# Order of the split products in the expert blocks, and branch hints from the fourteenth block on

## The chip, the cores and the metric

The kernel runs on one core of a Trainium2 chip, as one program. The metric is the time of one execution on the device in microseconds; a version is told by the median of its runs. A profiled execution gives the span from its first to its last instruction and the rows that are quoted here. The engines are TensorE (PE for its products, PEld for its weight loads), VectorE (DVE), ScalarE (ACT), GpSimd (POOL) and SyncE (SP, which issues most DMAs). A "q" behind an engine's name means its sequencer, which waits, branches and issues.

## The reference

Three layers follow each other. The attention has no softmax; each score goes through a sigmoid.

```
scores = scale * q @ k.T - log(S)            # 4 batches, 12 heads, 448 x 64
x = sigmoid(scores) @ v                      # then reshaped to 1792 tokens x 768
idx = argmax over 8 experts of cosine(x, expert_emb) / tau;  gate = its softmax weight
for e in range(8):                           # w1[e]: 768 x 1024, w2[e]: 1024 x 768
    m = idx == e
    x2[m] = gate[m] * (relu(x[m] @ w1[e]) @ w2[e])
out = ((x2 @ w_a) * (x2 @ w_b)) @ w_out      # 768 x 1536, 1536 x 768
```

Which expert a token goes to is known only when the kernel runs.

## The kernel before

Every product of full precision is made from three products of TensorE in a shorter format: each operand is split into a high and a low part (`split`, lines 759 to 761: ScalarE copies the high part, VectorE subtracts it from the operand to get the low part), and high x high, high x low and low x high are summed in PSUM.

The work has three stages. The attention (`attention`) runs over batches and pairs of heads and, beside them, routes the tokens to experts. The expert stage (`moe`) works on blocks of 128 tokens of one expert each. The last stage (`glu`) multiplies groups of 512 tokens by `w_a`, `w_b` and `w_out`; its rows carry the names `ab` and `o`. The order in which every engine gets its instructions is that of the Python text.

The tokens come in two phases of 896, so 14 blocks at least are live, and a phase can need more, up to 28 in all: every expert rounds its tokens up to full blocks. Blocks 0 to 13 always run. Each later block stands in a `tc.If` on the value `live`, nested in the block before it (`block`, line 979); `live` is loaded into a register on all engines a block ahead. In the profiled execution 18 blocks run: 288 weight loads per kind of product at line 906, 16 to a block. Where the first block is not live, each engine branches to the arm for that case, takes a few semaphore steps there, and branches on to the code of the last stage.

One block (`block1`) does this on TensorE:

- `p1_half`, twice: 18 products of 512 columns for one half of `h` (lines 820 to 822), a ReLU on ScalarE (line 823). In the second one, after four of six steps, `h_tr(b, 0)` transposes the first turn of `h` (line 869) into PSUM, and ScalarE and VectorE make `hTh` and `hTl`, its high and low parts, from it.
- `p2`, the second product: for each of eight slices `kk`, three kinds of products with two column halves each: `hTh` x `w2h`, `hTh` x `w2l`, `hTl` x `w2h` (line 906, tile `p`). Between its slices stand `h_tr(b, 1)`, the transposes of the second turn of `h`, which gives the other four slices of `hTh` and `hTl`, and `x_load(b + 1)`, which transposes the next block's tokens (line 756).
- Where the next block has another expert (`chg`), the splits of its `w1` are issued behind `x_load`, four of the eight splits of `w2` behind this block, and the other four in the next block, around its two `p1` (`was_new`). Block 0 splits the last four slices of its own `w2` behind its `x_load`.
- VectorE scales the two halves of `p` by the gate into `y` (line 949), and GpSimd scatters `y` to memory (line 955).

In `glu`, `y_tr` transposes the tokens of the first group (line 756, tile `py`), ScalarE and VectorE split them into `yh` and `yl`, and the first `ab` products (lines 1071 to 1073) need those and the split weights `whi` and `wlo`. Beside all stages a preparation of `w_a`, `w_b`, `w_out` runs in small units (`prep_tick`, lines 195 to 212).

Of the kernel before, what the change touches and what calls it, by code (L numbers as in the profile page):

```python
# [20 lines left out]
ENGINES = [ET.SP, ET.Activation, ET.DVE, ET.PE, ET.Pool]  # L21
# [3 lines left out]
def build(ctx: ExitStack, tc: tile.TileContext, q, k, v, emb, tau, w1, w2, wa, wb, wo, out, dbg=None, stop=None):  # L25
# [16 lines left out]
    KF = DF // P  # L42
# [183 lines left out]
    def prep_tick(dma=nc.sync, behind=0):  # L226
        prep_store(dma)
        prep_finish(behind)
        prep_load(next_unit[0] + 3, dma)
        prep_unit()  # L230
# [220 lines left out]
    def pump(ps=(True, LATE, END)):  # L451

        while bg:
            job = next((j for j in bg if j[2]), bg[0])
            if job[1] and job[1] not in ps:
                return
            job[2] = False
            try:
                job[1] = next(job[0])
                return  # L460
            except StopIteration:
                bg.remove(job)
# [300 lines left out]
    def fl(b, row):  # L763
        ph = 0 if b < LIVE0 else 1
        return flg[ph][0:1, row, b - TB[ph][0]:b - TB[ph][0] + 1]

    def value(b, row, mx, engines):
        return nc.values_load(fl(b, row), engines=engines, min_val=0, max_val=mx)

    def load_w(which, expert, pair):  # L770
        t, src = (r1[pair], w1) if which == 1 else (r2[0][:, 2 * pair:2 * pair + 2, :], w2)
        nc.sync.dma_start(out=t, in_=src[expert, 2 * pair * P:2 * (pair + 1) * P, :].rearrange("(k p) c -> p k c", p=P))

    def split_w(which, kk, pool=None):
        hi, lo = (w1h, w1l) if which == 1 else (w2_t["h"], w2_t["l"])
        t = r1[kk // 2][:, kk % 2, :] if which == 1 else r2[0][:, kk, :]
        split(hi[kk], lo[kk], t, hi[kk].bitcast(F32))

    def gather(b):
        if b >= NBLK:  # L780
            return
        ph = 0 if b < LIVE0 else 1
        t = xg_t[b % len(xg_t)]
        j = b - TB[ph][0]
        nc.gpsimd.indirect_dma_start(out=t, out_offset=None, in_=xs_d[:CAP[0], :] if ph == 0 else xs_d[:, :],
                                     in_offset=bass.IndirectOffsetOnAxis(ap=idx[ph][:, j:j + 1], axis=0))
        xg[b] = t
# [26 lines left out]
    def p1_half(b, hf, ps, h, inner, at=4):  # L814
        xh, xl = xT_[b]
        cs = slice(hf * FH, (hf + 1) * FH)
        for kk in range(KD):
            if kk == at:
                inner()
            nc.tensor.matmul(ps, lhsT=xh[:, kk, :], rhs=w1h[kk][:, cs], start=kk == 0, stop=False)  # L820
            nc.tensor.matmul(ps, lhsT=xh[:, kk, :], rhs=w1l[kk][:, cs], start=False, stop=False)  # L821
            nc.tensor.matmul(ps, lhsT=xl[:, kk, :], rhs=w1h[kk][:, cs], start=False, stop=kk == KD - 1)  # L822
        nc.scalar.activation(out=h, in_=ps, func=AF.Relu)
        hs_of.setdefault(b, []).append(h)
# [40 lines left out]
    def h_tr(b, hf):  # L865
        px = misc["ps"]()
        n = FH // P
        for kk in range(n):
            nc.tensor.transpose(out=px[:, kk * P:(kk + 1) * P], in_=hs_of[b][hf][:, kk * P:(kk + 1) * P],
                                identity=ident)  # L870
        ks = slice(hf * n, (hf + 1) * n)
        split(hT["h"][:, ks, :], hT["l"][:, ks, :], px.rearrange("p (k c) -> p k c", k=n),
              hT["h"][:, ks, :].bitcast(F32))

    def moe(r2_p):
        pool = moe_pool
        w2h, w2l, hTh, hTl = w2_t["h"], w2_t["l"], hT["h"], hT["l"]
        mx_p = pool("mx", 2)
        r2.append(r2_p.tile([P, KF, DM], F32, name="r2"))
        ps_1 = pool("ps_1", 2, space=PSUM)  # L880
        ps_2 = pool("ps_2", 2, space=PSUM)
        ps_x = pool("ps_x", 4, space=PSUM)
        misc["ps"] = lambda: ps_x.tile([P, 512], F32, tag="px", name="px")
        def block1(b, chg, was_new, load, e_load):
            def when_new(fn, chg=chg):
                if chg is not None:
                    with tc.If(chg == 1):
                        fn()

            def load_new(which):  # L890
                for i in range((KD if which == 1 else KF) // 2):
                    load_w(which, e_load, i)

            def split_new(which, k0, k1):
                for kk in range(k0, k1):
                    split_w(which, kk)

            def p1(hf, inner):
                p1_half(b, hf, ps_1.tile([P, FH], F32, tag="p1", name="p1"),
                        mx_p.tile([P, FH], F32, tag="h", name="h"), inner)  # L900

            def p2(yp, k0, k1):
                for kk in range(k0, k1):
                    for l, wv in ((hTh, w2h), (hTh, w2l), (hTl, w2h)):
                        for hf in range(2):
                            nc.tensor.matmul(yp[hf][:, :HD], lhsT=l[:, kk, :], rhs=wv[kk][:, hf * HD:(hf + 1) * HD],  # L906
                                             start=kk == 0 and wv is w2h and l is hTh,
                                             stop=kk == KF - 1 and l is hTl)

            def tick():  # L910
                if b < LIVE:
                    pump()
                    pump()

            if b > 0:
                when_new(lambda: load_new(1), load)
                p1(0, lambda: None)
                when_new(lambda: split_new(2, KF // 2, KF - 2), was_new)
                tick()

                def rest():
                    h_tr(b, 0)
                    when_new(lambda: split_new(2, KF - 2, KF), was_new)

                p1(1, rest)
                tick()
                if b < LIVE - 1:
                    prep_tick(behind=1)
                when_new(lambda: load_new(2), load)
            yp = [ps_2.tile([P, 512], F32, tag="p2", name="p2") for _ in range(2)]  # L930
            p2(yp, 0, 1)
            h_tr(b, 1)
            p2(yp, 1, 2)
            x_load(b + 1)
            if b == 0:
                split_new(2, 4, KF)
                when_new(lambda: load_new(1), load)
                when_new(lambda: load_new(2), load)
            when_new(lambda: split_new(1, 0, KD))
            p2(yp, 2, KF // 2)  # L940
            gather(b + 2)
            tick()
            if 0 < b < LIVE - 1:
                prep_tick(behind=1)
            p2(yp, KF // 2, KF)
            tick()
            y = mx_p.tile([P, DM], F32, tag="y", name="y", bufs=1)
            for hf in range(2):
                nc.vector.tensor_scalar(out=y[:, hf * HD:(hf + 1) * HD], in0=yp[hf][:, :HD],
                                        scalar1=slots[:, 2, b:b + 1], scalar2=None, op0=ALU.mult)  # L950
            when_new(lambda: split_new(2, 0, KF // 2))
            ph = 0 if b < LIVE0 else 1
            j = b - TB[ph][0]

            nc.gpsimd.indirect_dma_start(out=ys_d if b < LIVE else ys_d[:Y0, :], out_offset=bass.IndirectOffsetOnAxis(ap=idy[ph][:, j:j + 1], axis=0),
                                         in_=y, in_offset=None)

        for i in range(2, KF // 2):
            load_w(2, e_of[0], i)

        def block(b, was_new=None):
            nx = b + 1
            if nx < NBLK:
                if b + 2 >= LIVE0:
                    while bg:
                        pump()
                chg = value(nx, 1, 1, [ET.Activation, ET.DVE, ET.Pool])
                load = value(b + 2, 3, 1, [ET.SP])
                e_load = value(b + 2, 4, E - 1, [ET.SP])
                live = value(nx, 0, 1, ENGINES) if nx >= LIVE else None  # L970
            else:
                chg = load = e_load = None
            block1(b, chg, was_new, load, e_load)
            if nx == LIVE:
                first_loads()
            if nx < LIVE:
                block(nx, chg)
            elif nx < NBLK:
                with tc.If(live == 1):
                    block(nx, chg)  # L980

        block(0)
        moe_s.close()

# [222 lines left out]
```

## Time and profile before

| what | value |
|---|---|
| median of 3 runs | 1097.88 us (1095.52 to 1099.14) |
| the profiled execution's own time | 1095.02 us |
| its span, first to last instruction | 1093.3 us |
| TensorE busy with products | 1063.3 us, 97% of the span |
| VectorE, ScalarE, GpSimd busy | 595.8, 501.3, 152.5 us |
| mean granted clock of TensorE, as a share of full speed | 0.995 |

Busy shares are means over stages with different limits. A row of a wait tells which engine stood and whose result ended it; the idle time of an engine other than the one that sets the end costs nothing by itself. Products on TensorE overlap, so the distance from one row to the next tells more than the length in a row.

### The profile page before, as it was taken

The page shows a single profiled execution, that of the slowest core. Times are in us where ns is not written, and L with a number is a line of the kernel's source. Part 1 is how long each engine was busy: PE and PEld are TensorE (multiplying, and loading weights), DVE is VectorE, ACT ScalarE, POOL GpSimd, SP SyncE. Part 2 cuts the span into 40 slices and gives each one's busy share as a digit, 9 for nine tenths or more (in the row PEclk, how much of TensorE's full clock was granted, in tenths as well). Part 3 has the DMA queues.
Part 4 walks back from the last instruction along what each step waited for, and adds up shares of the span by engine and source line. Part 5 has one row for each costly group of instructions (what it writes and reads, how often), then busy time and mean ns, then how long its engine had stood idle before and what let it go on. Part 6 is the DMA issues. An engine that isn't in the chain of part 4 may idle for free.

```text
span 1093.3 us, 16706 instructions
## 1 busy us (share of the span) xinstructions
PE 1063.3 (97%) x5996; PEld 866.6 (79%) x5996; DVE 595.8 (54%) x1037; ACT 501.3 (46%) x761; POOL 152.5 (14%) x218
## 2 busy tenths in 40 slices
PE   7999999999999999999979999999999999999998
PEld 4555555599888888888968878888888888888997
DVE  2566788865883879271255996433333433333553
ACT  5777777442763676261243554332323322323443
POOL 2121322232121212131101331000000000000000
PEclk9999999999999999999989999999999999999999
DMA  6687687539658865722182665064221162220730
GB/s 164 168 210 204 174 237 213 197 138 338 243 211 305 326 226 211 299 82 110 45 287 67 245 213 230 1 242 177 87 87 44 59 268 107 88 87 1 317 132 29
DMA packets 116744, 187.69 MB, mean 172 GB/s; under 512 B 53784, under 2 KB 88856, under 8 KB 110624
## 3 DMA queue, kind: packets, MB, share of 16 engines
q1 hardware_dynamic: 112000, 171.10, 46.6%
q0 software_dynamic: 3040, 14.94, 3.7%
q8 instruction: 49, 0.80, 0.3%
q10 hardware_dynamic: 1600, 0.39, 0.2%
q14 instruction: 55, 0.45, 0.1%
HBM read 154.17 MB, written 32.24 MB: 170 GB/s over the span
## 4 chain that ended last, share of the span: by engine, by line
PE 43%; DVE 3%; DMA 2%; issue 1%; ACT 1%; POOL 0%; SPq 0%; ACTq 0%; DVEq 0%; POOLq 0%
PE ab L1071 10%; PE ab L1072 9%; PE ab L1073 9%; PE o L1104 5%; PE o L1105 5%; PE o L1106 5%; DVE wlo L761 1%; DMA wx<-wm 1%; DVE m L195 1%; DMA r<-wm 1%; PE ab L756 0%; DVE wx L212 0%; ACT whi L760 0%; DVE m L197 0%; POOL m L202 0%
## 5 line engine op out<-in xcount | busy, mean ns | idle before, releaser
L1071 PE MATMUL ab<-yh,whi 128*128 128x512 f32 (+1 forms) x576 | 210.2, 365 | 4.0 <-DVE m L1079 2.1
L1072 PE MATMUL ab<-yl,whi 128*128 128x512 f32 (+1 forms) x576 | 209.6, 364 | 0.0
L1073 PE MATMUL ab<-yh,wlo 128*128 128x512 f32 (+1 forms) x576 | 209.5, 364 | 0.0
L202 POOL TENSOR_TENSOR m<-m,raw 128x384 int32<-128x384 int32 x72 | 76.2, 1059 | 369.0 <-DVE m L197 162.4
L1071 PEld LDWEIGHTS ab<-yh,whi 128*128 128x128 f32 x576 | 109.2, 190 | 20.2 <-DVE m L1079 2.5
L1073 PEld LDWEIGHTS ab<-yh,wlo 128*128 128x128 f32 x576 | 109.1, 189 | 17.4 <-DVE wlo L761 0.2
L1072 PEld LDWEIGHTS ab<-yl,whi 128*128 128x128 f32 x576 | 109.1, 189 | 15.7
L1104 PE MATMUL o<-whi,gh 128*128 128x512 f32 x336 | 114.7, 341 | 0.0
L1105 PE MATMUL o<-whi,gl 128*128 128x512 f32 x336 | 113.9, 339 | 0.0
L1106 PE MATMUL o<-wlo,gh 128*128 128x512 f32 x336 | 112.9, 336 | 0.0
L1079 DVE TENSOR_TENSOR m<-ab,a 128x512 f32<-128x512 f32 (+1 forms) x48 | 30.0, 624 | 149.8 <-PE ab L1073 149.7
L760 ACT CAST gh<-m 128x512 fp32r<-128x512 f32 (+1 forms) x48 | 27.2, 567 | 173.6 <-DVE m L1079 173.6
L557 ACT ACTIVATE a<-ps,bias_s 128x896 f32<-128x896 f32 x96 | 92.7, 1004 | 27.4 <-PE ps L552 26.6
L761 DVE TENSOR_TENSOR wlo<-wx,whi 128x768 fp32r<-128x768 f32 x72 | 66.0, 972 | 46.8 <-ACT whi L760 46.7
L761 DVE TENSOR_TENSOR wlo<-r,whi 128x768 fp32r<-128x768 f32 x70 | 65.0, 984 | 45.9 <-ACT whi L760 45.9
L820 PE MATMUL p<-w1h,xh 128*128 128x512 f32 x216 | 86.2, 399 | 0.1
L822 PE MATMUL p<-w1h,xl 128*128 128x512 f32 x216 | 84.7, 392 | 0.0
L821 PE MATMUL p<-w1l,xh 128*128 128x512 f32 x216 | 84.4, 391 | 0.0
L906 PE MATMUL p<-w2h,hTl 128*128 128x384 f32 x288 | 74.1, 338 | 7.2 <-DVE hTl L761 7.2
L574 PE MATMUL av<-a,v 128*64 128x448 f32 (+1 forms) x384 | 78.4, 565 | 1.5 <-DVE xtok L590 1.5
L906 PE MATMUL p<-w2h,hTh 128*128 128x384 f32 x288 | 76.3, 346 | 0.0
L760 ACT CAST whi<-wx 128x768 fp32r<-128x768 f32 x72 | 55.4, 833 | 41.8 <-PE o L1105 35.5
(236 smaller groups left out, 1830.2 us busy)
## 6 DMA issues: line engine op xcount, KB each, us to landing
wx<-wm SPq DMA_DIRECT2D x22, 1152.0 KB, 12.3
r<-wm SPq DMA_DIRECT2D x21, 1152.0 KB, 7.1
r<-in_moe_w_dram SPq DMA_DIRECT2D x28, 768.0 KB, 7.6
r<-in_moe_w_dram SPq DMA_DIRECT2D x18, 1024.0 KB, 9.2
raw<-in_moe_w_a_dram SPq DMA_DIRECT2D x24, 384.0 KB, 5.1
raw<-in_moe_w_b_dram SPq DMA_DIRECT2D x24, 384.0 KB, 4.6
raw<-in_moe_w_out_dram SPq DMA_DIRECT2D x24, 384.0 KB, 3.5
wm<-ab SPq DMA_DIRECT2D x48, 192.0 KB, 5.6
```

What stands on the lines that cost most here:

```text
L557: nc.scalar.activation(out=a[r], in_=ps[:n, :, :S], func=AF.Sigmoid, bias=bias_s[:n], scale=qscale)
L761: eng.tensor_tensor(out=lo, in0=src, in1=f32_hi, op=ALU.subtract)
L820: nc.tensor.matmul(ps, lhsT=xh[:, kk, :], rhs=w1h[kk][:, cs], start=kk == 0, stop=False)
L821: nc.tensor.matmul(ps, lhsT=xh[:, kk, :], rhs=w1l[kk][:, cs], start=False, stop=False)
L822: nc.tensor.matmul(ps, lhsT=xl[:, kk, :], rhs=w1h[kk][:, cs], start=False, stop=kk == KD - 1)
L906: nc.tensor.matmul(yp[hf][:, :HD], lhsT=l[:, kk, :], rhs=wv[kk][:, hf * HD:(hf + 1) * HD], start=kk == 0 and wv is w2h and l is hTh, stop= ...
L1071: nc.tensor.matmul(ps[:, :n], lhsT=hi[:, s, cs], rhs=yh[:, kk, :n], start=kk == 0, stop=False)
L1072: nc.tensor.matmul(ps[:, :n], lhsT=hi[:, s, cs], rhs=yl[:, kk, :n], start=False, stop=False)
L1073: nc.tensor.matmul(ps[:, :n], lhsT=lo[:, s, cs], rhs=yh[:, kk, :n], start=False, stop=kk == KD - 1)
L1104: nc.tensor.matmul(t[:, d0:d1], lhsT=gh[:, cs], rhs=hi[:, 2, d0:d1], start=first, stop=False)
L1105: nc.tensor.matmul(t[:, d0:d1], lhsT=gl[:, cs], rhs=hi[:, 2, d0:d1], start=False, stop=False)
L1106: nc.tensor.matmul(t[:, d0:d1], lhsT=gh[:, cs], rhs=lo[:, 2, d0:d1], start=False, stop=last)
```

## The change

It has two parts. The slices of `p2` are issued in another order: in each half of four slices, all products with `hTh` come first and those with `hTl` behind them; `h_tr(b, 1)` stands behind the `hTh` products of two slices, `x_load` behind those of a third. And from the block on that the first conditional block follows, each engine gets a hint instruction at the start of a block, which names the branch at the block's end and gives the register `live` as what it will do; the `tc.If` names the body as the way that falls through.

```
-            def p2(yp, k0, k1):
+            def p2(yp, k0, k1, part=slice(0, 3)):
                 for kk in range(k0, k1):
-                    for l, wv in ((hTh, w2h), (hTh, w2l), (hTl, w2h)):
+                    for l, wv in ((hTh, w2h), (hTh, w2l), (hTl, w2h))[part]:
...
-            p2(yp, 0, 1)
+            p2(yp, 0, 2, slice(0, 2))
             h_tr(b, 1)
-            p2(yp, 1, 2)
+            p2(yp, 2, 3, slice(0, 2))
             x_load(b + 1)
...
             when_new(lambda: split_new(1, 0, KD))
-            p2(yp, 2, KF // 2)
+            p2(yp, 3, KF // 2, slice(0, 2))
+            p2(yp, 0, KF // 2, slice(2, 3))
             gather(b + 2)
...
-            p2(yp, KF // 2, KF)
+            p2(yp, KF // 2, KF, slice(0, 2))
+            p2(yp, KF // 2, KF, slice(2, 3))
...
                 live = value(nx, 0, 1, ENGINES) if nx >= LIVE else None
+                if live is not None:
+                    tc.mark_branch_hint_location(f"live{nx}", live, ENGINES)
...
             elif nx < NBLK:
-                with tc.If(live == 1):
+                with tc.If(live == 1, label=f"live{nx}", preferred_fallthrough_block=True):
                     block(nx, chg)
```

## Rows read from the trace of the kernel before

**Rows 1.** Waits, whole expert stage: who waited for whom, us in total, times, longest.
```profile
PE p L906 <- DVE hTl L761: 7.2, 6, 1.8
```
**Rows 2.** Timeline, 407 to 412: start, us, engine, line, operation, tiles, count, idle before.
```profile
407.70 0.51 PE L906 MATMUL p<-w2h,hTh 128*128 128x384 f32 x2
...
408.51 0.60 ACT L823 ACTIVATE h<-p 128x512 f32<-128x512 f32 x1
...
409.92 0.62 PE L906 MATMUL p<-w2h,hTl 128*128 128x384 f32 x2 [1.36 <-DVE hTl L761]
410.37 0.60 PE L869 MATMUL px<-ident,h 128*128 128x128 f32 x4
```
**Rows 3.** Windows of two pairs: length, then PE, PEld, DVE, ACT, POOL busy, clock, DMA.
```profile
410.65:429.21 18.56, 17.52 (x95) 15.65 (x93) 18.42 (x26) 16.04 (x24) 4.57 (x4) 1.00 0.70 268
296.28:315.72 19.44, 18.54 (x98) 16.22 (x98) 19.30 (x26) 14.81 (x22) 4.57 (x4) 1.00 0.73 277
```
**Rows 4.** Timeline, 426 to 430.6.
```profile
426.19 0.59 ACT L760 CAST hTh<-px 128x512 fp32r<-128x512 f32 x1 [0.50 <-PE px L869]
...
428.14 0.60 ACT L823 ACTIVATE h<-p 128x512 f32<-128x512 f32 x1
...
430.40 0.38 PE L869 MATMUL px<-ident,h 128*128 128x128 f32 x2
```
**Rows 5.** Timeline, 308.5 to 317.
```profile
308.89 0.56 ACT L201 ACTIVATE ab<-raw 128x384 f32<-128x384 bf16 x1 [3.10 <-DMA wm<-ab]
...
312.93 0.66 PE L869 MATMUL px<-ident,h 128*128 128x128 f32 x4 [0.76 <-ACT h L823]
...
316.17 0.61 ACT L823 ACTIVATE h<-p 128x512 f32<-128x512 f32 x1
...
316.91 0.27 PE L869 MATMUL px<-ident,h 128*128 128x128 f32 x1
```
**Rows 6.** Timeline of three other blocks.
```profile
372.29 0.61 PE L906 MATMUL p<-w2h,hTl 128*128 128x384 f32 x2 [1.38 <-DVE hTl L761]
...
484.20 0.59 ACT L823 ACTIVATE h<-p 128x512 f32<-128x512 f32 x1
...
485.39 0.60 PE L869 MATMUL px<-ident,h 128*128 128x128 f32 x4
...
223.69 3.57 DVE L761 TENSOR_TENSOR w2l<-r,w2h 128x768 fp32r<-128x768 f32 x4
...
228.63 0.39 PE L820 MATMUL p<-w1h,xh 128*128 128x512 f32 x1
```
**Rows 7.** Line 979, VectorE, 540 to 560: ns min/median/max, first and last start.
```profile
L979 DVEq COMPARE_BRANCH  x2: 47/52/56, 549.0 to 552.2; - x2
L979 DVEq EVENT_SEMAPHORE  x2: 21/21/21, 552.0 to 552.1; - x2
```
**Rows 8.** The chain that ended last, 548 to 557: start, us, what.
```profile
552.28 2.15 issue
```
**Rows 9.** Timeline, 547 to 563.
```profile
547.05 0.51 PE L906 MATMUL p<-w2l,hTh 128*128 128x384 f32 x2
547.39 0.51 PE L906 MATMUL p<-w2h,hTl 128*128 128x384 f32 x2
...
552.14 2.46 PE L756 MATMUL py<-ident_r,raw 128*128 128x128 f32 x21 [2.73 <-issue]
...
554.83 1.95 DVE L761 TENSOR_TENSOR yl<-py,yh 128x384 fp32r<-128x384 f32 x4 [5.92 <-ACT whi L760]
...
556.46 0.77 PE L1071 MATMUL ab<-yh,whi 128*128 128x512 f32 x1 [1.86 <-DVE yl L761]
...
562.45 0.59 ACT L1076 COPY a<-ab 128x512 f32<-128x512 f32 x1 [2.07 <-issue]
```
**Rows 10.** Window behind the expert stage, columns as in the third group.
```profile
554.00:559.50 5.50, 3.64 (x12) 2.80 (x12) 4.67 (x11) 5.17 (x11) 0.00 (x0) 0.50 1.03 397
```
**Rows 11.** Timeline, 655 to 658.
```profile
656.60 0.50 PE L1071 MATMUL ab<-yh,whi 128*128 128x512 f32 x1 [2.10 <-DVE m L1079]
```

## The prediction

> **What bounds the kernel now.** I read the page first: one execution spans 1093.3 us, its own time is 1095.02 us, and TensorE is busy for 97% of the span, so a change can only pay where TensorE stands still or runs at its lower clock. Then I listed TensorE's idle stretches from the first expert block to the end, by its timeline, and by the waits view who ended them. There are three kinds. In the expert blocks, six waits for `hTl`, 7.2 us together, the longest 1.8 [rows 1]. Behind the last two expert products (547.39+0.51, so 547.9) a gap of 8.5 us with only 24 transposes in it, up to the first GLU product at 556.46 [rows 9]. And one wait of 2.1 us in the GLU stage, at 656.60 [rows 11], in lines that the diff doesn't touch. So the prize is bounded: 7.2 us in the blocks, and some 8 us and the slow clock behind them.
>
> *The waits in the blocks.* In block 410 (blocks are named by the time of their wait) the products `p` begin at 407.70; where nothing is awaited, rows of two stand 0.34 to 0.35 us apart (547.05 and 547.39 [rows 9]), so a product takes 0.174. The first with `hTl` waits 1.36 us, and the transposes of the second turn of `h` come at 410.37, although `h` itself was done at 408.51+0.60=409.11 [rows 2]. VectorE makes `hTl` late because it still splits the new expert's weights: all six waits stand in blocks that follow a change of expert.
>
> *The gap behind the blocks.* Here the code of line 979 is the thing to read. VectorE's branch past the dead blocks starts at 549.0 (2 rows: 549.0 and 552.2) and takes 0.06 us; its next instruction, the semaphore step of the not-taken arm, is at 552.0 [rows 7]. The chain of waits then has 2.15 us of "issue" at 552.28, behind VectorE's second branch: no semaphore is waited for, the instruction is simply not there [rows 8]. TensorE, idle for 2.73 us, goes on at 552.14, just behind that step, ScalarE with it, VectorE's `yl` starts at 554.83, TensorE's first `ab` product at 556.46 [rows 9]. [...] So two fetches of code on VectorE, 2.9 and 2.2 us, set the start of the GLU stage.
>
> **The change, part by part.** *New order of the products.* Nothing is added: 48 products a block before and after, each with its own weight load, the two PSUM tiles in the same alternation. Eight products with `hTh` (instead of four, and two with `hTl`) stand ahead of the transposes `h_tr(b, 1)`, and the first `hTl` product comes behind 16 others and both sets of transposes, some 3.5 us into the stage. A block without a wait gains nothing: x_load keeps its place, 12 products in, and the gather its place behind the first 24. In a block with a wait, the transposes can start when the eight products are done or `h` is there (with 0.1 us of hand-over, as from 552.0 to 552.14), whichever is later, and two products more, 0.35 us, are then behind them. A restart costs up to 0.1 us per step (0.45 us from 409.92 to 410.37 where 0.35 is the rule); I take 0.15.
>
> Block 410: eight products end at 409.09, `h` gives 409.21; against 410.37 that is 1.16+0.35-0.15=1.4 us. But what is late next? Block 430 changes expert again, and from 410.65 to 429.21 VectorE is busy for 18.42 of 18.56 us [rows 3]. Its work doesn't come sooner when TensorE does, so what block 410 gains, TensorE would stand at 430. There `h` sets the end: 428.14 on ScalarE, less the 0.50 us that ScalarE waited for TensorE at 426.19, so 427.64+0.60+0.10=428.34 against 430.40 [rows 4]: 2.06+0.35-0.15=2.3 us for the two blocks together. Blocks 296 and 316 are such a pair too, VectorE busy for 19.30 of 19.44 us [rows 3]. There a store held ScalarE for 3.10 us at 308.89, TensorE waits for its `h` at 312.93 already, and the second `h` ends at 316.17+0.61=316.78 whatever TensorE does; the transposes now start at 316.91 [rows 5]: 0.03+0.35, 0.4 us. Block 372, with a wait of 1.38 us [rows 6], has no change of expert behind it: 1.4 us, as 410 by itself. Block 485: 484.20+0.59+0.10=484.89 against 485.39 [rows 6]: 0.50+0.35-0.15=0.7 us. One block loses: in block 0 the last four `w2l` are made while they are used, 3.57 us from 223.69, 0.89 each [rows 6]. Six products per `kk` take 1.04 us and stay behind that; four take 0.69 and overtake it. The last `w2l` is there at 227.26; two products and eight with `hTl`, 10x0.174, end at 229.0, and the next block now starts at 228.63 [rows 6]: a loss of 0.4 us. Sum: 0.4+1.4+2.3+0.7-0.4=4.4 us. Bounds: 7.2 us above [rows 1]; below 1.7, if both pairs give nothing.
>
> *The hints.* From the fourteenth block on there is one instruction more per block on each engine, and five of them execute. No row shows it. Nearest are VectorE's branches and semaphore steps, 0.02 to 0.06 us [rows 7], so 0.3 us on a queue; the other end is the 2.9 us that a branch waits for its code, should the instruction itself wait so. I take nothing, by the nearer rows: these blocks have no wait of TensorE except the one at 485, so VectorE and ScalarE have idle time that covers it. Without the cover it is 0.3 us.
>
> *What the hint is worth* if the code of the not-taken arm is there when VectorE branches: its semaphore step comes at 549.2, not 552.0, and the second branch at 549.4. [...] Then ScalarE starts `yh` at 549.3, and VectorE its `yl` one copy of 0.5 us later, at 549.85, and from `yl` to the first product it is 1.63 us, as now: 551.5, 5.0 us sooner. Late next is VectorE: from the point at which TensorE starts it still has two `wlo` and four `yl` to make, some 3.1 us (four take 1.95 [rows 9]), and TensorE at full clock would be there after 2.3: a wait of 0.8. In return the clock: the first 18 products take 6.0 us now (556.46 to 562.45, where ScalarE copies them); at full clock a product of 512 columns takes 0.213+0.014=0.227 (384 columns: 0.160 of the 0.174), 18 of them 4.1, with the wait 4.9. TensorE's idle stretches would be 1.3 and 0.4 us; the 1.36 us in block 410 left the clock at 1.00 [rows 2, 3], the 2.73 us before 552.14 did not, and these are nearer to the first. So 1.0 us for the clock, and 6.0 in all. Bounds: 0, and 7.4 us (556.46 less 549.05, the branch itself). What TensorE gains here it keeps, since VectorE's work in the GLU stage is started by TensorE's products.
>
> Together 4.4+6.0=10.4 us: 1095.0 becomes 1084.6. The profiled execution is 2.9 us under the median of the runs, 1097.88, so the median comes to **1087.5 us**.
>
> [...] The row at 552.28 shows an engine that waits for code behind a branch [rows 8]. [...] No row here has a hint in it.
>
> **The rivals.** *1. Only the first fetch goes.* For it: the gaps are two, and the second stands with the arm's code already there. `yl` starts 2.55 us behind the second branch (552.28 to 554.83), so at 549.4+2.55=551.95, 2.9 us sooner; TensorE would be idle for some 2.4 us before it, near the 2.73 that cost the clock and far from the 1.36 that didn't; half of the clock's 1.0 counts. 3.4+4.4=7.8 us: 1090.1.
>
> *2. The hint does nothing*, only the order counts: 1093.5. For it: no row shows code that comes ahead of a branch. Against it: the branch's value is known a whole block ahead.
>
> [...]
>
> **How the numbers follow.** Chances: forecast 0.43, rival 1 0.25, rival 2 0.20, rival 3 0.12. The forecast's own spread is some 3 us either way, from the pairs and the clock. The range takes in rivals 1 and 2 and the better part of the bound of 7.2 us in the blocks: **1083.5 to 1095.0**; left out are rival 3 and a tail, some 0.18. 0.3% is 3.3 us, about what a measurement of this kernel can tell from no change. Faster by that: forecast, rival 1 and half of rival 2, 0.78. Within it: the other half and a little of rival 3, 0.13. Slower: 0.09.
>
> **What would show it.** Right: no wait for `hTl` in blocks 296 to 485, waits for `h` in its place, large only in the second block of each pair; some 0.4 us for `w2l` in block 0; VectorE's step of the not-taken arm within 0.3 us of its branch, TensorE's first `ab` product 3.6 us behind the last expert product, and the granted clock at 1.00 through it. Wrong: still 3 us behind VectorE's branch (rival 2), 2 us behind its second (rival 1), or new idle time of TensorE in the last five blocks (rival 3). The sum also fails if the 2.1 us wait in the GLU stage grows by what its start gains.

## The result and the profile after

The changed kernel takes 1087.30 us (median of 4 runs, 1084.99 to 1090.51), the kernel before, run beside it, 1096.88 (4 runs, 1095.52 to 1099.14): a ratio of 0.9906, 95% interval 0.9884 to 0.9928. The forecast was 1087.5. That the sum came out does not make its terms right, so the terms come next.

The profiled execution of the changed kernel took 1089.07 us and spans 1087.31, that of before 1095.02 and 1093.31: 6.0 us apart, where the medians are 9.6 apart. By stage (from TensorE's timeline of both: first expert product with `w2h`, end of the last one, 19th `ab` product, end of the span) the 6.0 us are +1.31 ahead of that first product, -4.09 in the expert stage, -4.88 from there to the 19th `ab` product and +1.66 in the rest of the GLU stage. The change touches the two in the middle, 9.0 us against the 10.4 forecast. The two others go with stretches at the lower level of TensorE's clock (0.50), as the windows show (length, busy time of PE, PEld, DVE, ACT, POOL, granted clock, DMA):

```profile
548.10:551.30 3.20, 3.20 (x16) 2.60 (x15) 3.20 (x8) 3.20 (x9) 0.00 (x0) 0.50 0.84 281
551.50:554.50 3.00, 3.00 (x14) 2.44 (x14) 2.78 (x6) 1.24 (x2) 0.00 (x0) 1.00 0.97 393
650.50:653.70 3.20, 3.20 (x9) 2.53 (x8) 3.13 (x7) 3.19 (x6) 1.12 (x1) 0.50 0.44 181
...
201.00:206.00 5.00, 5.00 (x20) 2.90 (x22) 3.51 (x14) 1.48 (x2) 1.02 (x1) 0.50 0.02 9
```

The last window lies ahead of the experts; before, the clock was back at 1.00 there by 204.8. In the one from 650.5 TensorE runs nine products where at full clock it runs sixteen (in `b0_old`, below, over the same time). It stands behind the wait of [rows 11], which is 2.11 us now and was 2.10; before, the clock stayed at 1.00 behind it. The fourteen profiles of this study (before, after and twelve experiments) sort cleanly by it: the first product with `w2h` comes at 219.0 to 219.5 us where the low stretch ahead of the experts lasts 3.4 us, at 220.4 to 220.9 where it lasts 6.8; the rest of the GLU stage takes 531.1 to 531.2 us without a low stretch and 532.7 to 533.0 with one, whatever the change in the code.

*The blocks.* The waits view of the expert stage, to hold against [rows 1]:

```profile
PE px L869 <- ACT h L823: 1.1, 3, 0.5
PE px L869 <- ACTq L887: 1.0, 1, 1.0
PE p L821 <- DVE w1l L761: 0.3, 2, 0.2
```

No wait for `hTl` is left of the 7.2 us; beside them, before, stood 0.8 us for `h` (312.93 in [rows 5]). Now 2.4 us stand under other names, the largest a new one of 1.05 us in a block that had waited for nothing before, at 351.13. The timeline there:

```profile
339.48 0.56 ACT L199 ACTIVATE raw<-raw 128x384 int32<-128x384 uint32 x1 [0.17 <-ACTq L887]
349.12 0.55 ACT L201 ACTIVATE ab<-raw 128x384 f32<-128x384 bf16 x1 [9.08 <-DMA wm<-ab]
350.48 0.60 ACT L823 ACTIVATE h<-p 128x512 f32<-128x512 f32 x1 [0.82 <-ACTq L887]
...
351.13 0.66 PE L869 MATMUL px<-ident,h 128*128 128x128 f32 x4 [1.05 <-ACTq L887]
```

ScalarE stands for 9.08 us in front of its step `ab<-raw` (line 201, which prepares the GLU weights) until a store has landed, starts `h` 0.82 us behind that step, and TensorE waits for `h`. It is the kind of wait of [rows 5].

*The hand-over.* The timeline that answers to [rows 9], and VectorE's branch line (983 now) to hold against [rows 7]:

```profile
545.83 0.42 PE L756 MATMUL py<-ident_r,raw 128*128 128x128 f32 x3 [0.70 <-PEq L983]
547.02 2.38 PE L756 MATMUL py<-ident_r,raw 128*128 128x128 f32 x21 [0.78 <-PE py L756]
...
547.04 1.69 ACT L760 CAST yh<-py 128x384 fp32r<-128x384 f32 x4 [7.59 <-DVEq L983]
...
547.73 1.95 DVE L761 TENSOR_TENSOR yl<-py,yh 128x384 fp32r<-128x384 f32 x4 [1.60 <-ACT yh L760]
...
549.37 0.77 PE L1075 MATMUL ab<-yh,whi 128*128 128x512 f32 x1
...
554.54 0.39 PE L1075 MATMUL ab<-yh,whi 128*128 128x512 f32 x1
```

```profile
L983 DVEq COMPARE_BRANCH  x2: 61/70/79, 546.3 to 547.1; - x2
L983 DVEq EVENT_SEMAPHORE  x2: 21/21/21, 546.9 to 547.0; - x2
```

The step of the not-taken arm comes 0.6 us behind the start of the first branch, not 3.0, and `yl` starts 0.6 us behind the second branch, not 2.6. That code was on its way in both waits of before is in the trace: of the DMA packets of the kind `instruction` (on the page, 49 of 16 KB on one queue, 55 of up to 8 KB on another) one of 16 KB starts between 549.0 and 549.5 and two of 8 KB between 550.0 and 550.5, in the first wait, and one of 8 KB between 552.3 and 553.0, in the second. In the changed kernel none moves from 544.2 to 547.2, and two of 8 KB do between 547.26 and 547.73. For which engine a packet is, the trace does not tell. The last expert product ends at 545.13; the first `ab` product follows 4.24 us later (8.56 before), the 19th, at 554.54, 9.41 us later (14.29 before).

### The profile page after: what moved, and what is told of

It is laid out like the page before. It is cut to its first block, busy times and chain, and to the rows that moved or that the text cites. A ratio compares the mean times of both kernels' runs of the same rounds, so it can differ in the third digit from the quotient of the medians.

```text
span 1087.3 us, 16743 instructions
## 1 busy us (share of the span) xinstructions
PE 1066.4 (98%) x5996; PEld 866.6 (80%) x5996; DVE 594.7 (55%) x1037; ACT 501.5 (46%) x761; POOL 152.9 (14%) x218
## 4 chain that ended last, share of the span: by engine, by line
PE 44%; DVE 3%; DMA 2%; ACT 1%; issue 0%; POOL 0%; SPq 0%; ACTq 0%; POOLq 0%
PE ab L1075 10%; PE ab L1076 10%; PE ab L1077 10%; PE o L1108 5%; PE o L1109 5%; PE o L1110 5%; DVE wlo L761 1%; DMA wx<-wm 1%; DVE m L195 1%; DMA r<-wm 1%; PE ab L756 0%; DVE wx L212 0%; PE py L756 0%; ACT whi L760 0%; DVE m L197 0%
## 5 line engine op out<-in xcount | busy, mean ns | idle before, releaser
L760 ACT CAST whi<-wx 128x768 fp32r<-128x768 f32 x72 | 55.4, 832 | 44.2 <-PE o L1109 36.3
L760 ACT CAST whi<-r 128x768 fp32r<-128x768 f32 x70 | 53.8, 832 | 47.0 <-PE o L1109 42.5
```

Source lines behind the costliest of these rows:

```text
L760: nc.scalar.copy(out=hi, in_=src)
```

## The experiments

All ratios are to the kernel before on the same chip, with 95% intervals. In the tables, a block's length is the distance between the first `w2h` products of two blocks, and the hand-over goes from the end of the last expert product to the first `ab` product, both from TensorE's timeline.

**Each half by itself.** `order_only` is the changed kernel without the hints and with the plain branch; `hints_only` is the kernel before with them.

```diff
# order_only
-                if live is not None:
-                    tc.mark_branch_hint_location(f"live{nx}", live, ENGINES)
-                with tc.If(live == 1, label=f"live{nx}", preferred_fallthrough_block=True):
+                with tc.If(live == 1):
```

> The new order of the products alone, no hints. Theory (two parts that add up, the order worth about 4.1 us as the profile after the change shows it, the hints about 5): 1092.5 to 1093.5 us against some 1097, ratio about 0.996; the waits for hTl gone, the stage of the expert blocks some 4 us shorter, and the gap behind the last block as before: VectorE's next instruction 2.9 us behind its branch at the last live block, 2.2 us behind the next branch, 8.5 us from the last expert product to the first ab product. Rival (the order also shortens the gap, for instance by moving code): the gap under 7 us, ratio 0.993 or less.

> The hints alone, with the old order of the products. Theory: about 5 us less, ratio about 0.9955; six waits for hTl as before (7.2 us together), 4.3 us from the last expert product to the first ab product, VectorE's next instruction within 0.6 us of its branch. Rival (the hints cost something in the blocks, which the order hides): ratio 0.998 or more, new idle time of TensorE in the last five blocks.

`order_only`: 0.9943 (0.9927 to 0.9958), 1092.08 us. `hints_only`: 0.9951 (0.9937 to 0.9966), 1092.06 us. The product, 0.9894, lies within the interval of the two together, 0.9884 to 0.9928: the halves add, and neither is idle. The profiles part them cleanly. `order_only` has an expert stage of 324.58 us (changed kernel 324.72, before 328.80) and a hand-over of 8.69; `hints_only` has 328.66 and 4.24, and its waits view still has the six waits:

```profile
PE p L906 <- DVE hTl L761: 8.3, 6, 1.8
```

**Which hint counts.** `hint_dve_only` gives the hint to VectorE alone, `hint_not_dve` to every engine but VectorE, `hint_18_only` to all engines but only ahead of the first dead block.

```diff
# hint_dve_only
-                    tc.mark_branch_hint_location(f"live{nx}", live, ENGINES)
+                    tc.mark_branch_hint_location(f"live{nx}", live, [ET.DVE])
# hint_not_dve
+                    tc.mark_branch_hint_location(f"live{nx}", live, [e for e in ENGINES if e != ET.DVE])
# hint_18_only (and the plain branch for the other blocks)
-                if live is not None:
+                if nx == 18:
```

> The changed kernel, but the hint on VectorE alone. Theory (VectorE's two fetches of code set the start of the last stage, those of the other engines are hidden): within 1 us of the changed kernel, 1087 to 1088.5, although ScalarE, TensorE and SyncE still wait 2 to 4 us for code behind their branches. Rival (the late code of TensorE or ScalarE would be the next limit, just behind VectorE's): the first ab product 1 to 3 us later than in the changed kernel, 1088.5 to 1090.5.

> The changed kernel, but with one hint only, for the branch that is not live in this data (block 18), so that the code of each engine grows by one hint in front of that branch and not by one per block. Theory A (the hint brings the arm's code and what follows it): both of VectorE's waits for code are gone, 1087 to 1088. [...]

> The hint stays on four engines and is taken from VectorE alone. Theory A (the hand-over behind the experts is set by VectorE's two waits for code, and by nothing that the hint does on the other engines): VectorE's branch past the dead blocks is followed only some 2.9 us later and its second branch some 2.2 us later, as before the change (2.92 and 2.15), the first ab product comes some 8.5 us behind the last expert product instead of 4.24, and the time is that of the order alone, about 1092. Rival B (the hints on TensorE, ScalarE or SP also give something, or move code of VectorE): one of VectorE's two waits is gone or shorter, hand-over 6 us or less, 1087 to 1090.

`hint_dve_only`: 0.9890 (0.9875 to 0.9906), hand-over 4.24. (The 2 to 4 us of its text, in the trace of the kernel before: ScalarE's step of the arm comes 4.2 us behind its branch, 542.8 to 547.0, SyncE's 2.4, 505.6 to 508.0, and TensorE's branch takes 3.6.) `hint_18_only`: 0.9886 (0.9871 to 0.9902), hand-over 4.24. Both are the whole effect: the hint for one branch of five is enough, and so is VectorE's hint alone. `hint_not_dve` came out between its two expectations: 0.9929 (0.9908 to 0.9949), hand-over 6.75. VectorE's branch line there:

```profile
L983 DVEq COMPARE_BRANCH  x2: 47/52/56, 545.1 to 548.1; - x2
L983 DVEq EVENT_SEMAPHORE  x2: 21/21/21, 547.9 to 548.0; - x2
```

The first wait is back, from 545.1 to 547.9. The second is not, `yl` starting at 548.68 behind the branch at 548.1. So the first wait goes only with VectorE's own hint, and the second had gone for some other reason. Two runs look for it.

**What removes the second wait.** `fall_only` has no hint and keeps the named arm of the branch; `hint_no_fall` has the hints and not the named arm.

```diff
# fall_only
-                if live is not None:
-                    tc.mark_branch_hint_location(f"live{nx}", live, ENGINES)
# hint_no_fall
-                with tc.If(live == 1, label=f"live{nx}", preferred_fallthrough_block=True):
+                with tc.If(live == 1, label=f"live{nx}"):
```

> No hint instruction at all; the branches past the dead blocks keep what else the change gave them (the not-taken arm named as the one to fall through to). Theory F (VectorE's second wait for code goes by that, not by the hint; the run with the hint on every engine but VectorE lost only the second): VectorE's first branch is followed 2.8 to 3.1 us later, the second 0.15 us later, first ab product 6.5 to 7 us behind the last expert product, about 1089.5. Theory A (the hint on any engine is needed for it, or the code's place in memory): both waits are there, 2.9 and 2.15 us, hand-over 8.5, about 1092.

> The hints stay on all engines; the not-taken arm is no longer named as the one to fall through to. Theory F: the first branch of VectorE is followed 0.56 us later, its second 2.15 us later, first ab product some 6.3 to 6.8 us behind the last expert product, about 1089.5. Theory A (the hint brings the arm's code and what follows it): both waits gone, 0.56 and 0.16, hand-over 4.24, 1087.

`fall_only`: 0.9960 (0.9943 to 0.9977), hand-over 8.95, VectorE's waits 3.17 and 2.29 us. `hint_no_fall`: 0.9900 (0.9880 to 0.9919), hand-over 4.24, waits 0.56 and 0.16. Theory F falls: the named arm does nothing that these runs show. With `finish0` (below), which has all hints, the second wait was back, in a program whose VectorE executes its steps in the blocks in another order; the chain that ended last shows it as [rows 8] do:

```profile
543.21 0.06 DVEq L983
543.27 2.14 issue
545.41 0.05 DVEq L761
```

In the fourteen kernels profiled (before, after and twelve experiments) the first wait is 0.5 to 0.6 us in all ten in which VectorE has the hint and 2.8 to 3.2 in the four others. The second is 0.15 to 0.16 us in ten, and 2.14 to 2.29 in four: before, `order_only`, `fall_only`, and `finish0`. It follows neither the hint on VectorE (`hint_not_dve` is without it and does not wait, `finish0` has it and waits) nor the named arm. Three of the four have no hint on any engine: were it not for `finish0`, a hint on any engine would be enough to explain it. That the place of the code decides would fit all fourteen, but no run moved the code alone: it was not shown, and stays open.

**What is left in the blocks.** The new wait at 351 and those for `h` pointed to ScalarE's wait for the store. Three kernels try to take that away: `store_act` and `store_pool` issue these stores from ScalarE's and from GpSimd's queue instead of SP's; `finish0` has VectorE finish a prepared piece one tick earlier. In the order as it is, a tick first stores the piece that the tick before finished, then finishes the piece begun two ticks earlier, then begins a new one. With three buffers for `ab`, the new piece takes the buffer whose store was issued in the same tick. With the earlier finish that store was issued a tick before.

```diff
# store_act (store_pool: nc.gpsimd), at both ticks of a block
+                    prep_store(nc.scalar)
                     prep_tick(behind=1)
# finish0, at both ticks of a block
-                    prep_tick(behind=1)
+                    prep_tick()
```

> In the expert blocks the stores of the prepared weights (wm<-ab) are issued by ScalarE's queue instead of SP's, where they stand behind the new expert's weight loads. Theory S (what is left of TensorE's waits in the blocks, 1.05 us in block 352 and some 1.2 us for h and w1l in the pairs, comes from ScalarE standing still in front of its step ab<-raw until such a store has landed): ScalarE's waits for wm<-ab in the blocks, 29.3 us in 8 of them, fall to under 5 us, the wait at 351 goes, and the expert stage is 1 to 2 us shorter than the 324.7 of the changed kernel; time 1085 to 1086.5. Rival V (VectorE is the bound of the blocks that change their expert, and ScalarE's waits are only covered work): ScalarE's waits go, TensorE's stay within 0.3 us, under another releaser, 1087. Rival C (the earlier stores take bandwidth from the weight loads): TensorE waits longer for w1l or w2l, 1088 or more.

> The same stores are issued by GpSimd's queue instead of SP's. Theory S: as with ScalarE's queue, ScalarE's waits for wm<-ab fall from 29.3 us to under 5, the expert stage is 1 to 2 us shorter than 324.7, 1085 to 1086.5. Rival G (GpSimd, which makes the sum m and issues the gather and the scatter, is late with one of them because of the stores that it now issues): a wait of TensorE for xg or of VectorE for m appears, and the gain is gone, 1087 to 1089.

> In the expert blocks the prepared weights are finished (VectorE's step ab<-ab,m) one tick earlier, so that their store can leave one tick earlier too and no longer leaves in the very tick in which ScalarE needs its buffer. Theory S (what is left of TensorE's waits in the blocks comes from ScalarE standing still in front of ab<-raw until the store of that tick has landed): ScalarE's waits for wm<-ab in the blocks fall from 29.3 us to under 8, the wait at 351 and most of the waits for h go, the expert stage is 323.0 to 324.0 us, time 1085.5 to 1086.5. Rival G: VectorE, whose step now stands one tick nearer to GpSimd's sum, waits for m in the blocks in which it is the bound, and TensorE waits 1 us or more for w1l, w2l or hTl in a block that changes its expert: stage 325 or more, 1088 or more.

(The 29.3 us of these texts are the kernel before's; the changed kernel has 36.3 us in 9 waits.) `store_act` is far slower, 1.0369 (1.0351 to 1.0388), 1138.99 us. None of its three theories had that. ScalarE's timeline in one of the six blocks:

```profile
303.81 0.60 ACT L823 ACTIVATE h<-p 128x512 f32<-128x512 f32 x1
309.80 0.33 ACTq L224 DMA_DIRECT2D wm<-ab  x1
310.17 0.54 ACT L199 ACTIVATE raw<-raw 128x384 int32<-128x384 uint32 x1 [5.76 <-DMA r<-in_moe_w_dram]
315.47 0.54 ACT L201 ACTIVATE ab<-raw 128x384 f32<-128x384 bf16 x1 [4.76 <-DMA wm<-ab]
```

The store needs VectorE's step `ab<-ab,m` (307.03, 0.55 us long). ScalarE, done with `h` at 304.41, has no other row until it issues the store at 309.80 (the last 2.2 us of that are not explained), and starts `ab<-raw`, after 4.76 us of waiting for the store to land, at 315.47. `hTh` comes behind that, at 315.91, and TensorE stands 5 to 8 us in each of six blocks. The stage is 51.5 us longer than the changed kernel's: around each wait the granted clock is at 0.50 for 6.8 to 10.2 us (its mean over the profiled run is 0.974, where the changed kernel has 0.994), and the waits themselves are

```profile
PE p L906 <- ACT hTh L760: 42.3, 6, 8.3
```

`store_pool`: 0.9939 (0.9924 to 0.9954), 1090.66 us, expert stage 326.70. Here the store stands behind GpSimd's sum and gather (at 303.84 behind 301.66 and 302.82), and ScalarE's waits for it grow from 36.3 us in 9 to 61.8 in 14. Of rival G the place was wrong (no wait of VectorE for `m` or of TensorE for `xg`); the gain is gone, as it said, and the time is 1.7 us beyond its range.

`finish0`: 0.9891 (0.9872 to 0.9909), 1085.47 us; the ratios alone don't tell it from the changed kernel (0.9884 to 0.9928). ScalarE has no wait for a store left in the blocks, and TensorE's waits there are down to one line, the third of the changed kernel's:

```profile
PE p L821 <- DVE w1l L761: 0.3, 2, 0.2
```

The expert stage is 320.91 us, 3.8 shorter than the changed kernel's and more than theory S had (323 to 324); the second wait that came back took 1.9 us of it in the hand-over (6.17), and the first 18 `ab` products 0.8 us more (6.00). The block lengths (us) show where the 3.8 came from. The kernels of the changed order with the stores as they were (the second to fourth column, and five more that are not shown) differ among themselves by up to 1.6 us in each pair and in the block at 351; the two without ScalarE's waits (but for one of 0.2 us in `best18`) agree within 0.1 in all three:

```
                    before  after  hint_not_dve  hint_18_only  store_pool  finish0  best18
block 0              19.13  19.67         19.67         19.68       19.67    19.68   19.13
pair 296/316         39.67  37.77         39.19         38.12       38.98    36.80   36.73
block at 351         18.20  19.28         18.02         19.58       17.99    18.01   17.99
block 372            19.63  18.14         18.13         18.15       18.66    18.08   18.08
pair 410/430         39.67  38.35         38.24         37.95       39.91    36.80   36.76
block 485            18.92  18.13         18.13         18.13       18.11    18.13   18.13
all 17.5 blocks     328.80 324.72        324.78        325.02      326.70   320.91  320.24
```

In those eight kernels the last step `ab<-raw` that ScalarE does in a block sets the end of two of these blocks. Block 296 ends 5.96 to 5.98 us behind the start of that step in every one of them: 13.18 us into the block and a length of 19.16 in the changed kernel, 14.61 and 20.59 in `hint_not_dve`. The block at 351 ends 3.9 us behind it, and takes 18.0 where the step starts by 14.1 us or has nothing to wait for. Counted from the first expert product, the step that the block at 351 waits for starts at 128.3 to 129.5 us in all ten kernels with the stores on SP's queue and the late finish, the old order among them. So the order hardly moves it, and what TensorE gains in the blocks ahead it loses in part at 351.

**Block 0 in the old order.**

```diff
-            p2(yp, 0, 2, slice(0, 2))
+            new = b > 0
+            p2(yp, 0, 2, slice(0, 2)) if new else p2(yp, 0, 1)
...
```

> Block 0 keeps the old order of its products, all others the new one. By the prediction block 0 loses 0.4 us with the new order (four products per kk overtake the last w2l, which are made while they are used); the two profiles show 0.54. If that is the new order's, the stretch from block 0's first product to that of the next block falls from the changed kernel's value by 0.4 to 0.55 us to that of the kernel before, and so does the expert stage, 324.2 against 324.7; time 0.5 us under the changed kernel, about 1086.8, which the rounds can hardly tell. Rival: the end of block 0 is set by VectorE and ScalarE splitting w2 and w1 in either order, and the 0.54 us is given back or taken in the next block: the stretch changes by under 0.2 us.

1087.45 us, 0.9909 (0.9893 to 0.9925), as the changed kernel; half a microsecond can't be seen in the medians. In the profile it can. The end of block 0 in the changed kernel, and in `b0_old`:

```profile
220.41 0.51 PE L906 MATMUL p<-w2h,hTh 128*128 128x384 f32 x2
...
228.62 0.61 PE L906 MATMUL p<-w2l,hTh 128*128 128x384 f32 x2
229.07 1.57 PE L906 MATMUL p<-w2h,hTl 128*128 128x384 f32 x8
230.49 0.39 PE L820 MATMUL p<-w1h,xh 128*128 128x512 f32 x1
```

```profile
219.00 0.51 PE L906 MATMUL p<-w2h,hTh 128*128 128x384 f32 x2
...
228.55 0.39 PE L820 MATMUL p<-w1h,xh 128*128 128x512 f32 x1
```

10.08 us against 9.55, and the block's whole length 19.67 against 19.15: the loss is the new order's.

**Together.** `best18` takes the hint ahead of the first dead block alone, the old order in block 0, and the earlier finish.

> Three of the studied edits together: the hint for the first dead block alone, block 0 in the old order, the prepared weights finished one tick earlier. Additive parts: expert stage 320.9 (the earlier finish) less 0.5 (block 0), so 320.4 us. VectorE's second wait for code came back with the earlier finish (2.14 us, hand-over 6.17 instead of 4.24) although its own program is as long as before. Theory P (where the code happens to lie decides the second wait; this version has 13 instructions fewer on each engine): it may go, then hand-over 4.2, about 1083. Rival T (the earlier finish itself makes it, by what VectorE does in the last blocks): it stays at 2.1, hand-over 6.2, about 1085.

1084.52 us, 0.9865 (0.9841 to 0.9889): the lowest ratio of all, 0.4% under the changed kernel's, but the two intervals overlap by a little. Expert stage 320.24 (expected 320.4), hand-over 4.19, second wait 0.16. That the second wait went again speaks against rival T, since the earlier finish is still there, and is what theory P allowed; it does not show P.

## Why the forecast came out, and where its terms did not

*The order, 4.4 us forecast, 4.09 measured.* The mechanism was right: all six waits for `hTl` are gone, and in the blocks with a wait the transposes follow `h`. Its terms:

- Block 372: 1.4 forecast, 1.49 measured. Block 485: 0.7, and 0.79. Block 0: a loss of 0.4, and 0.54. These three repeat within 0.1 us wherever those blocks have the new order and the stores leave from SP's queue.
- The pair at 410: 2.3 forecast, 1.32 measured. The pair at 296: 0.4 forecast, 1.90 measured. What failed is the step in which VectorE's full load (18.42 of 18.56 us, [rows 3]) was taken to set the pair's length in the new order too. In `finish0` VectorE is as full (17.43 of 17.50 us from 296.9 to 314.4) and both pairs take 36.80 us, 2.9 less than before. In the changed kernel the bound is ScalarE's step behind the store, which in the pair at 296 starts 13.2 us in, before 14.7. Before, it was not: `hints_only`, in the old order, has it at 13.4 and the same 39.67 us. The forecast did take that store as the limit of the pair at 296, but as a fixed date; counted from the first expert product it comes 1.06 us earlier in the changed kernel, and 0.1 us earlier in `order_only`, where the pair gains 0.95. So a part of the 1.90 is the luck of one profile: over the eight kernels the pair at 296 gains 0.48 to 1.90 and the one at 410 1.32 to 2.60.
- The block at 351: nothing forecast, a loss of 1.08 measured. The wait of ScalarE was there before (7.92 us at 348.11) and hidden but for some 0.2 us; the forecast looked at what is late next in the blocks that had a wait, not in the others. The date of its step and `finish0` show the cause: without the wait for the store the block takes 18.01 us.

So the 4.09 is a sum of terms off by up to 1.5 us each way, and in other kernels of the same order the stage took 323.56 to 325.40 us.

*The hints, 6.0 us forecast, 4.88 measured.* That VectorE would find the not-taken arm's code at the branch is shown, to 0.6 us, by the pair `hint_dve_only` (branch at 546.0, step at 546.6) and `hint_not_dve` (545.1 and 547.9). Rival 2 is out by `hints_only`. The sign of rival 3, new idle time of TensorE in the last five blocks, is missing too: the two whole blocks behind the one at 485 take 18.01 us each, 18.03 before. Rival 1 did not happen to the changed kernel, but did to `finish0`, whose hand-over is 1.9 us longer. The forecast's `yl` at 549.85 takes the second wait as gone as well. That was the author's assumption, and no row of before shows it; the runs showed 0.15 to 0.16 us in its place in the changed kernel and nine others, and 2.14 in `finish0`. In `hint_not_dve` VectorE has no hint, and the second wait is gone as well. As far as the record goes, this part came out by luck. The hints' own cost, taken as nothing, is right: 0.03 to 0.06 us each (25 in the trace of the changed kernel, five on each engine), and the expert stage of `hints_only` is no longer than before (328.66 against 328.80).

Two sizes were off. The first `ab` product comes 4.24 us behind the last expert product, 3.6 forecast: a hinted branch is not free here, its arm comes 0.64 us behind the branch's start, where 0.15 was assumed, and `yl` starts 0.69 us behind `yh`, not 0.55. And the clock, at 0.50 behind the waits of before [rows 10]: it was to stay at 1.00, and fell to 0.50 from 548.0 to 551.4, so that 2.05 us of the 18 products stand at 0.50. It cost next to nothing there. The 18 products take 5.18 us, and 5.12 in `b0_old`, where the clock stays at 1.00 and TensorE waits for VectorE's `yl` instead:

```profile
546.40:548.00 1.60, 1.60 (x6) 0.98 (x7) 1.60 (x5) 1.60 (x6) 0.00 (x0) 1.00 1.06 422
```

```profile
546.32 0.47 PE L1082 MATMUL ab<-yh,whi 128*128 128x512 f32 x1 [0.40 <-DVE yl L761]
```

Where more of the stretch is at 0.50, it does cost. The fourteen kernels, by how much of the 18 products' time stands at 0.50 (us):

```
                                     at 0.50   18 products
five kernels (b0_old, best18, ...)  0 to 1.75  5.12
after, hint_18_only                 2.05-2.08  5.17-5.18
hint_not_dve                           2.30    5.27
hints_only                             2.80    5.50
before                                 3.32    5.74
hint_no_fall                           3.39    5.78
finish0                                3.83    6.00
order_only                             4.67    6.38
fall_only                              5.53    6.79
```

Up to some 2 us VectorE sets the pace; from there on, by these rows, each microsecond at 0.50 costs about half of one. So the forecast was right that the clock costs time here, and nearly right with VectorE's 4.9 us at full clock (5.12). Its 0.227 us for a product of 512 columns at full clock is the distance between products in the trace of before (twelve from 560.16 to 562.88); less the 0.174 for 384 columns that leaves 0.053 for 128, from which its 0.213 and 0.160 follow, and the 0.014 that is left. For its clock term the size was wrong: 1.0 forecast, 0.56 measured (5.74 to 5.18). Its 6.0 us for before ran to ScalarE's copy, 0.25 us behind the nineteenth product.

*The sum.* 8.97 us measured where 10.4 was forecast. The medians moved by 9.6, and the profiled pair by 6.0 only, since the stretches at 0.50 ahead of the experts and in the GLU stage took 3.0 us back there. These come and go from one execution to the next: among the runs of the kernel before are 1095.3 us at a mean clock of 0.995 and 1100.7 at 0.988.

## What to carry to other kernels

A block that seems set by a full engine may, once changed, be set by another: look at what the third engine waits for in the same block (here ScalarE, 9.08 us at 349.12, for a store that left too late to have landed), and before counting a gain, list the hidden waits of all blocks, not only of those that wait now. Where an engine stands for 2 to 3 us behind a branch with no semaphore awaited, hint that branch on that engine (here VectorE's 2.9 us became 0.6), and read in the profile whether its next branch still waits. A store moved to ScalarE's own queue made ScalarE wait for the data (`store_act`, 304.41 to 309.80).

## What was not expected of the hardware

- A hinted branch still cost VectorE 0.5 to 0.6 us to its next instruction, against 2.8 to 3.2 without the hint. One more instruction on each engine, on VectorE 17 us ahead of the branch (529.1 and 546.3 in the changed kernel), was enough for that (`hint_18_only`).
- The second wait, 2.1 to 2.3 us, appears in four kernels of fourteen: the three without any hint, and `finish0`. No single edit explains all of them.
- With nearly the same idle time of TensorE at the hand-over (0.70 to 0.80 and 0.68 to 0.78 us, with three transposes between) the granted clock fell to 0.50 in the changed kernel and in `hint_18_only`, `hints_only`, `hint_no_fall`, `finish0` and `store_act`, and stayed at 1.00 in `b0_old`, `best18` and `store_pool`. Behind the wait in the GLU stage (2.1 us, 1.8 in `hint_not_dve`) it fell in six kernels of fourteen. In these runs the idle time just ahead does not tell whether the clock falls.
